# GpSimd starts one operation per step behind a VectorE gate; VectorE applies the softmax reciprocal in the first batch

## The chip, the cores and the metric

The kernel runs on one core of one Trainium2 chip. The metric is device time in microseconds. The engines are named PE (TensorE, matmul), PEld (its weight loads), DVE (VectorE), ACT (ScalarE), POOL (GpSimd) and SP (SyncE, which only issues DMAs here).

## What is computed

```python
q_pool = q.reshape(B, H, S // 2, 2, D).mean(axis=3)          # B 4, H 8, S 1152, D 64
scores = scale * np.matmul(q_pool, k.transpose(0, 1, 3, 2))
attn = np.exp(scores - np.max(scores, axis=-1, keepdims=True))
attn = attn / (np.sum(attn, axis=-1, keepdims=True) + 1e-09)
x = heads_side_by_side(np.matmul(attn, v))                   # [4, 576, 512]
xn = (x - mu) / np.sqrt(var + 1e-06) * g_ln
out = x + np.maximum(xn @ w_ch1, 0.0) @ w_ch2                # w_ch1 512 x 2048, w_ch2 2048 x 512
```

All inputs and the output are fp32. The kernel gets near fp32 precision from fp16 matmuls by splitting each operand into a high and a low half.

## The kernel before

The attention is cut into 144 **steps**. A step takes 128 query rows of one pair of heads; nine steps make a pair (`C = 9`), four pairs a batch, so steps 0 to 35 are the first batch (`on_pe(i)` is true there). The order of the work is written by hand: `step(i)` issues the instructions of step `i` engine by engine, and each engine runs its own list in that order, waiting only on semaphores. The dictionary `todo` (filled with `at(i, ...)`) holds what is issued at the end of step `i`, `early` (`pre(i, ...)`) what is issued at its start.

In a step of the first batch DVE begins with the row maximum of the scores in PSUM (`emit_max`, L381), takes the reciprocal of the softmax sum of an earlier step (`evac_pv`, L512), and then runs what waits in the queue `fill`: three integer operations on a 128 x 512 block of the weights (`w_conv`, recorded through a helper as L109), which turn fp32 words into a scaled form in SBUF. It ends with the low halves of the next pair's K or Q (L283, L306), read from PSUM. ACT makes the exponential (L395), copies the transposed exponentials out of PSUM (L434), multiplies the product with V by the reciprocal (`two` in `evac_pv`, L519) and makes the high halves. PE computes the scores (L362, L370), adds up the weights' magnitudes (L732), transposes the exponentials (L428), multiplies them by V (L452) and turns the result back (L480).

POOL has four jobs in the first batch: it adds pairs of query rows (`pool_q`, L172) and copies them (`dup_q`, L178) for every second pair, copies V (`take_v`, L273), and turns converted weights into two fp16 halves. The last is `w_splits(part)`: the weights come in four parts of four slots, and each slot takes three operations, `w_split_a` (fp32 to fp32, L257), `w_split_b` (to fp16, L257) and `w_split_c` (a difference, L788). A part is split once its scale is known, and then an operation is issued every half step or so. Nothing but its operands holds POOL back, so it runs them one behind the other.

From step 36 on, the feed-forward part (L600, L632) runs beside the attention of the later batches, as far as the weights' parts have been split.

```python
def w_splits(part):
    for n in range(4):
        i0 = this[0] + 1 + 3 * n // 2 if part < 2 else 16 + 10 * part + 5 * n // 2
        for x, fn in ((0, w_split_a), (1, w_split_b), (2, w_split_c)):
            at(i0 + x, fn, 4 * part + n)
```

Of the kernel before, what the change touches and what calls it, by code (L numbers as in the profile page):

```python
# [9 lines left out]
FP32 = mybir.dt.float32  # L10
# [4 lines left out]
ALU = mybir.AluOpType  # L15
# [9 lines left out]
def tile_pooled_attention_moe(  # L25
# [18 lines left out]
    nc = tc.nc  # L44
# [4 lines left out]
    C = S // 128  # L49
    HP = H // 2  # L50
# [18 lines left out]
    sm_p = ctx.enter_context(tc.tile_pool(name="sm", bufs=2))  # L69
# [97 lines left out]
    def pool_q(p, eng, halves=None):  # L167

        a = raws[p, "q"]
        for o, n in ((0, 128),) if halves is None else halves:  # L170
            x = a[o:o + n].rearrange("p h c r d -> p (h c) r d")
            eng.tensor_tensor(x[:, :, 0], x[:, :, 0], x[:, :, 1], op=ALU.add)  # L172

    def dup_q(p, eng, halves=None):
        a = raws[p, "q"]
        for o, n in ((0, 128),) if halves is None else halves:
            x = a[o:o + n].rearrange("p h c r d -> p (h c) r d")
            eng.tensor_copy(x[:, :, 1], x[:, :, 0])  # L178
# [45 lines left out]
    reds, found = deque(), deque()  # L224
# [31 lines left out]
    def scaled(dst, src, s=1.0):  # L256
        nc.gpsimd.tensor_scalar(dst, src, s, 1.0, op0=ALU.mult, op1=ALU.mult)  # L257

    def take_v(p, h):

        st = pair[p]
        vr = raws[p, "v"]
        if "v" not in st:

            st["v"] = tr_p.tile([128, 2, C, 130], FP16, tag="v", name="vt")
            if on_pe(p * C):
                st["v"] = st["v"].bitcast(FP32)
                nc.gpsimd.memset(st["v"][:, :, :, 64:65], 1.0)
            else:
                nc.gpsimd.memset(st["v"][:, :, :, 64:66], 1.0)  # L270
        vt = st["v"][:, h]
        if on_pe(p * C):
            nc.gpsimd.tensor_copy(vt[:, :, 0:D], vr[:, h])  # L273
            return
        s = st["s"][:, 2:3]
        scaled(vt[:, :, 0:D], vr[:, h], s)
        scaled(vr[:, h], vr[:, h], s)
        nc.gpsimd.tensor_tensor(vt[:, :, 66:66 + D], vr[:, h], vt[:, :, 0:D], op=ALU.subtract)
# [57 lines left out]
    def on_pe(i):  # L336

        return 0 <= i < HP * C
# [133 lines left out]
    turned, scaled_out = deque(), deque()  # L472

    def emit_turn(n, ot, i):

        j = n % C
        ps = psum[:, 3 * (i % 2) + 2, 128:258]
        parts = [(h, 64 * h, 64) for h in range(2)] if j == 4 else [(0, 0, 128)]
        for h, q0, w in parts:
            nc.tensor.transpose(ps[0:w, 65 * h:65 * h + 65], ot[:, q0:q0 + w], ident[0:65, 0:65])  # L480
        one, two = evac_pv(n, ps)
        found.append(one)
        scaled_out.extend((two, lambda: evacuated(n)))

    pv_slot = [0]
    xb, xh = {}, {}
# [1 line left out]
    def evac_pv(i, ps):  # L488

        p, j = divmod(i, C)  # L490
        b, hp = divmod(p, HP)
        s = pair[p]["s"][:, 2:3]
        r = sm_p.tile([128, 2], FP32, tag="r", name="r", bufs=3)
        if j == 4:
            if b % 2 == 0 and hp == 0:
                xh[b // 2] = x_p.tile([128, 2, DM], FP32, tag="hh", name="xh")
            o, n, m = 64 * (b % 2), 64, 2
            x = xh[b // 2][o:o + n, 0, 128 * hp:128 * hp + 128]
        else:
            if j == 0 and hp == 0:  # L500
                room["x"] -= 4
                assert room["x"] >= 0
                xb[b] = x_p.tile([128, 4, DM], FP32, tag="xb", name="xb")
            h, t = PLACES[hp // 2][j]
            o, n, m = 0, 128, 1
            x = xb[b][:, t, 128 * hp + 64 * h:128 * hp + 64 * h + 64]
        r = r[o:o + n, 0:m]

        def one():
            sums = ps[o:o + n, 64:65 * m:65]  # L510
            if on_pe(i):
                nc.vector.reciprocal(r, sums)  # L512
            else:
                nc.vector.tensor_scalar(r, sums, EPS, s[o:o + n], op0=ALU.add, op1=ALU.mult)
                nc.vector.reciprocal(r, r)  # L515

        def two():
            for u in range(m):
                nc.scalar.activation(  # L519
                    out=x[:, 64 * u:64 * u + 64], in_=ps[o:o + n, 65 * u:65 * u + 64],  # L520
                    func=ACTF.Copy, scale=r[:, u:u + 1],
                )

        return one, two
# [269 lines left out]
    def at(i, fn, *a):  # L794
        todo.setdefault(i, []).append((fn, a))
# [3 lines left out]
    def pre(i, fn, *a):  # L799
        early.setdefault(i, []).append((fn, a))  # L800
# [5 lines left out]
    for p in range(1, NP):  # L806
        i0 = (p - 1) * C
        at(max(i0 - 1, 0), load, p, "k", nc.sync)
        at(i0, load, p, "v", nc.sync)
        at(i0 + 1, bound, p, "k")  # L810
        if p % 2 == 0:
            at(i0 - 2, load_q, p, (nc.sync,))
            pre(i0 + 1, pool_q, p, nc.gpsimd)
            at(i0 + 1, dup_q, p, nc.gpsimd)
            at(i0 + 2, bound, p, "q")
        elif p == 1:
            upper = (64, 64)
            pre(0, behind_scales)
            pre(i0 + 1, pool_q, 1, nc.gpsimd, (upper,))
            at(i0 + 1, dup_q, 1, nc.gpsimd, (upper,))  # L820
            at(i0 + 2, bound, 1, "q", *upper)
        else:
            at(i0 + 1, same_q, p)
        if not on_pe(p * C):
            at(i0 + 2, bound, p, "v")
        pre(i0 + 3, scales_reduce, p, 0, 2 if on_pe(p * C) else 3)
        for n in range(2):
            at(i0 + (5, 7)[n], take_v, p, n)
        for n, (fn, u) in enumerate(PREPS):
            late = 1 if on_pe(i0) else 0  # L830
            pre(i0 + 4 + n + late, lambda fn=fn, p=p, u=u: preps.append((fn, p, u)))

    for m in range(32):
        i0 = m
# [5 lines left out]

    this = [0]

    def w_splits(part):
        for n in range(4):
            i0 = this[0] + 1 + 3 * n // 2 if part < 2 else 16 + 10 * part + 5 * n // 2
            for x, fn in ((0, w_split_a), (1, w_split_b), (2, w_split_c)):
                at(i0 + x, fn, 4 * part + n)

# [62 lines left out]
    def evacuated(n):  # L911

        p, j = divmod(n, C)
        b = p // HP
        left[p] -= 1
        if not left[p]:
            pair.pop(p)
        key = ("h", b // 2) if j == 4 else (b, PLACES[p % HP // 2][j][1])
        whole[key] = whole.get(key, 0) + 1
        if whole[key] == 8 and key != ("h", 0):  # L920
            norms.append(key)
# [34 lines left out]
    def step(i):  # L956
        live = i < NSTEP
        this[0] = i
        for fn, a in early.pop(i, ()):
            fn(*a)  # L960
        if live:
            emit_max(i)
        if on_pe(i - 1):
            emit_t_copy(i - 1)
            steps.pop(i - 1)
        while found:
            found.popleft()()
        first = on_pe(i - 2) or on_pe(i)
        if first and not on_pe(i):
            a_piece(i)  # L970
        if on_pe(i):
            if i < 3:
                warm(16, bank())
            a_piece(i)
            a_prep()
            emit_exp(i)
        while scaled_out:
            scaled_out.popleft()()
        if i + 1 < NSTEP:
            emit_s(i + 1)  # L980
            pv_slot[0] = i + 1
        else:
            free_banks[:] = [6, 7, 0, 1, 3, 4]
            pv_slot[0] += 1
        while sums and i % 2 == sums[0][0] // 2:
            sums.popleft()[1]()
        if on_pe(i):
            while fill:
                drip()
            flush()  # L990
        else:
            flush()
            if live:
                emit_exp(i)
                emit_hi(i)
        if 0 <= i - 1 < NSTEP and not on_pe(i - 1):
            emit_lo(i - 1)
            steps.pop(i - 1)
            drip()
        norm(i)  # L1000
        while soon or len(fill) > 3:
            drip()
        if on_pe(i):
            emit_t(i)
            if reds:
                found.append(reds.popleft()())
        elif reds:
            evacs.append(reds.popleft()())
        while turned:
            n, ot = turned.popleft()  # L1010
            emit_turn(n, ot, i)
        if not on_pe(i):
            if not first:
                a_piece(i)
            some_units(i)
            a_prep()
        for fn, a in todo.pop(i, ()):
            fn(*a)

    def warm(n, ps=None):  # L1020
        ps = psum[:, 2, 0:128] if ps is None else ps[:, 0:128]
# [3 lines left out]
    with tc.manual_schedule():  # L1025
# [36 lines left out]
        one, two = all_max(st["acc"], 3, lambda ps: scales(0, ps, 0, 3, both=True))  # L1062
# [13 lines left out]
        i = 0  # L1076
# [32 lines left out]
```

## Time and profile before

| | |
|---|---|
| time, median of 3 runs | 882.64 us (880.32 to 884.50) |
| the profiled execution: its own time | 883.46 us |
| its span on the core | 881.7 us |
| PE, PEld busy | 823.7 us (93%), 587.6 us (67%) |
| DVE, ACT, POOL busy | 614.7 us (70%), 570.7 us (65%), 349.0 us (40%) |
| the same from 0 to 204 us (the start and the first batch) | PE 182.84, DVE 161.55, ACT 160.82, POOL 70.61 us |

A span is the time from the first to the last instruction on the core. An instruction's duration is what the profiler recorded; short instructions of one engine overlap by some tens of nanoseconds. Steps are told apart by their row maximum: a step lasts from one L381 to the next.

### The profile page before, as it was taken

What the parts mean: (1) busy time and instruction counts of PE and PEld (TensorE: products, weight loads), DVE (VectorE), ACT (ScalarE), POOL (GpSimd) and SP (SyncE); (2) the same over time, 40 slices, a digit from 0 to 9 for tenths busy, and PEclk for the clock granted to TensorE, in tenths of its full rate; (3) what the DMA queues carried; (4) which work ended last, traced back from release to release, by engine and by line L of the source; (5) the groups of instructions that cost most, each with busy time, mean ns of one, the idle gap of its engine ahead of it and who ended that gap; (6) DMA issues with size and microseconds to landing.
All of it is one profiled execution on the core that took longest, in us unless ns stands there. A gap on an engine that the chain in (4) does not pass through costs nothing.

```text
span 881.7 us, 21840 instructions
## 1 busy us (share of the span) xinstructions
PE 823.7 (93%) x9270; PEld 587.6 (67%) x9270; DVE 614.7 (70%) x1092; ACT 570.7 (65%) x851; POOL 349.0 (40%) x318
## 2 busy tenths in 40 slices
PE   8999899898898999898899999999999999999997
PEld 6778687686656575556666666566757576666764
DVE  4687989897777787778778777777877777532121
ACT  3988788887566686668676767676768676411110
POOL 3010634436776934364464345526343423300000
PEclk9999989899999999999999999999999999999999
DMA  6463436303589698969697969796988967600001
GB/s 187 149 207 120 129 120 183 120 1 87 105 146 181 129 173 162 201 132 181 118 222 124 196 126 215 125 179 113 196 155 158 175 113 135 121 13 13 16 10 24
DMA packets 276017, 115.97 MB, mean 132 GB/s; under 512 B 259280, under 2 KB 259280, under 8 KB 275920
## 3 DMA queue, kind: packets, MB, share of 16 engines
q1 hardware_dynamic: 275568, 113.70, 62.3%
q8 instruction: 72, 1.18, 0.5%
q10 hardware_dynamic: 352, 0.88, 0.4%
q14 instruction: 25, 0.20, 0.1%
HBM read 46.14 MB, written 4.72 MB: 58 GB/s over the span
## 4 chain that ended last, share of the span: by engine, by line
PE 51%; DVE 26%; ACT 13%; DMA 4%; issue 3%; POOL 1%; SPq 1%; ACTq 0%; POOLq 0%; DVEq 0%
PE psum L632 15%; PE psum L600 14%; DVE mx L381 7%; PE psum L464 6%; DVE hl L418 5%; PE psum L362 4%; PE psum L452 4%; ACT pe L395 3%; DVE stage L109 3%; DVE ht L614 2%; PE psum L428 2%; ACT ht L613 2%; DVE wsl L109 2%; PE psum L370 2%; DVE kt L283 1%
## 5 line engine op out<-in xcount | busy, mean ns | idle before, releaser
L381 DVE TENSOR_REDUCE mx<-psum 128x1 f32<-128x1152 f32 x144 | 194.4, 1350 | 20.6 <-ACT xb L519 7.0
L632 PE MATMUL psum<-wsl,ht 128*128 128x512 f16 x864 | 196.6, 379 | 3.9 <-DVE ht L614 3.4
L395 ACT ACTIVATE pe<-psum,nb,sc 128x1152 f32<-128x1152 f32 x144 | 188.9, 1312 | 12.0 <-DVE nb L386 10.5
L600 PEld LDWEIGHTS <-wsl 128*128 128x128 f16 x1920 | 171.9, 99 | 29.5 <-issue 9.2
L600 PE MATMUL psum<-xn,wsl 128*128 128x256 f16 x1536 | 181.7, 277 | 8.4 <-DVE xb L645 4.3
L632 PEld LDWEIGHTS <-ht 128*128 128x128 f16 x864 | 80.8, 98 | 92.3 <-issue 4.5
L409 ACT ACTIVATE hl<-pe 128x1152 f16<-128x1152 f32 x108 | 125.6, 1163 | 8.0 <-DMA pt<-hl 4.7
L362 PE MATMUL psum<-kt,qt 64*128 64x512 f16 (+1 forms) x960 | 127.4, 381 | 1.7 <-ACT pe L395 0.9
L614 DVE SCALAR_TENSOR_TENSOR ht<-psum,ht 128x512 f16<-128x512 f32 x72 | 49.8, 691 | 104.7 <-ACT ht L613 104.7
L464 PE MATMUL psum<-vt,pt 128*128 128x65 f16 (+1 forms) x3240 | 117.6, 194 | 0.0
L464 PEld LDWEIGHTS <-pt 128*128 128x128 f16 (+1 forms) x3240 | 109.5, 100 | 2.5 <-DMA pt<-hl 0.4
L418 DVE SCALAR_TENSOR_TENSOR hl<-pe,hl 128x1152 f16<-128x1152 f32 x72 | 109.3, 1518 | 0.0
L519 ACT ACTIVATE xb<-psum,r 128x64 f32<-128x64 f32 x128 | 39.7, 310 | 96.1 <-DVE r L515 89.0
L613 ACT ACTIVATE ht<-psum 128x512 f16<-128x512 f32 x72 | 42.7, 593 | 88.2 <-PE psum L600 87.9
L257 POOL TENSOR_SCALAR pe<-pe 128x1152 f32<-128x1152 f32 x36 | 42.0, 1168 | 140.1 <-ACT hl L409 135.4
L416 POOL TENSOR_TENSOR hl<-pe,hl 128x1152 f16<-128x1152 f32 x36 | 85.5, 2374 | 3.0
L452 PE MATMUL psum<-pt,vt 128*65 128x128 f32 (+1 forms) x720 | 82.1, 272 | 1.4 <-DVE qt L283 1.4
L452 PEld LDWEIGHTS psum<-pt,vt 128*65 128x65 f32 x720 | 76.1, 144 | 1.8 <-DVE qt L283 1.8
L362 PEld LDWEIGHTS <-qt 64*128 64x128 f16 (+1 forms) x960 | 39.8, 97 | 39.7 <-issue 22.3
L370 PEld LDWEIGHTS <-qt 128*128 128x128 f16 (+1 forms) x320 | 17.8, 99 | 72.5 <-issue 72.0
L370 PE MATMUL psum<-kt,qt 128*128 128x128 f16 (+1 forms) x320 | 41.4, 226 | 12.1 <-ACT xb L519 10.6
L283 DVE SCALAR_TENSOR_TENSOR qt<-psum,s,qt 128x384 f16<-128x384 f32 x48 | 29.5, 614 | 33.3 <-ACT qt L286 33.2
(116 smaller groups left out, 1003.8 us busy)
## 6 DMA issues: line engine op xcount, KB each, us to landing
stage<-in_moe_w_ch_dram SPq DMA_DIRECT2D x32, 512.0 KB, 5.1
kr<-in_k_dram SPq DMA_DIRECT2D x16, 576.0 KB, 4.5
qr<-in_q_dram SPq DMA_DIRECT2D x31, 288.0 KB, 6.2
vr<-in_v_dram SPq DMA_DIRECT2D x15, 576.0 KB, 4.7
out_dram<-xb SPq DMA_DIRECT2D x32, 128.0 KB, 2.5
pt<-hl SPq DMA_TRANSPOSE x108, 4.9
kr<-in_k_dram SPq DMA_DIRECT2D x16, 64.0 KB, 4.2
vr<-in_v_dram ACTq DMA_DIRECT2D x1, 576.0 KB, 6.7
```

The lines of the kernel that those rows point to most:

```text
L362: nc.tensor.matmul(out=sp[o:o + w, c0:c0 + 512], lhsT=qt[r:r + 64, qa, q0:q0 + w], rhs=kt[r:r + 64, ka, h], start=(a == 0), stop=(a == 2),)
L370: nc.tensor.matmul(out=sp[o:o + w, 1024:1152], lhsT=qt[:, qa, q0:q0 + w], rhs=pair[p]["k8"][:, h], start=(qa == 0), stop=(qa == 1),)
L381: nc.vector.tensor_reduce(mx, st["s"], axis=AX.X, op=ALU.max)
L395: nc.scalar.activation(out=st["pe"], in_=st["s"], func=ACTF.Exp, scale=pair[i // C]["sc"][:, 0:1], bias=st["nb"],)
L409: nc.scalar.activation(out=hl[:, 0], in_=st["pe"], func=ACTF.Copy, scale=2.0 ** 15)
L416: nc.gpsimd.tensor_tensor(hl[:, 1], st["pe"], hl[:, 0], op=ALU.subtract)
L418: nc.vector.scalar_tensor_tensor(hl[:, 1], st["pe"], 2.0 ** 15, hl[:, 0], op0=ALU.mult, op1=ALU.subtract)
L452: nc.tensor.matmul(out=ps[0:65, q0:q0 + w], lhsT=vt[:, h, c], rhs=pt[:, 128 * u + q0:128 * u + q0 + w], start=(u == 0), stop=(u == C - 1),)
L464: nc.tensor.matmul(out=dst[:, 0:n], lhsT=lhsT, rhs=rhs, start=(u == 0 and lhsT is hi and n == 65), stop=(u == C - 1 and lhsT is lo), skip_ ...
L600: nc.tensor.matmul(out=ps[:, o:o + n], lhsT=wsl[:, 8 * w + cc, wa, f * 128:f * 128 + 128], rhs=xn[:, xa * KD + cc, 0:n], start=(m == 0), s ...
L614: lambda: nc.vector.scalar_tensor_tensor(lo, pv, 0.0, hi, op0=ALU.max, op1=ALU.subtract),
L632: nc.tensor.matmul(out=ps, lhsT=hv[0][:, ha, f, t * 128:t * 128 + 128], rhs=wsl[:, 8 * w + 4 + f // 2, wa, (f % 2) * DM:(f % 2) * DM + DM] ...
```

## The change

`gate()` is new: DVE writes one column of a small tile and POOL copies it to the next column. POOL runs in order, so what stands behind the copy on POOL starts only after DVE has come to that place. Four such tiles are used in turn.

```diff
+    def gate():
+        x = sm_p.tile([128, 2], FP32, tag="gate", name="gate", bufs=4)
+        nc.vector.memset(x[:, 0:1], 1.0)
+        nc.gpsimd.tensor_copy(x[:, 1:2], x[:, 0:1])
```

The splits of the weights' first two parts go into a queue, `calm`. At the end of each step up to 34 one gate and one operation of the queue are issued; from step 35 on two operations and no gate. The splits of parts 2 and 3 start three to four steps later. In the first batch the query addition and copy also go through the queue, ahead of the rest, their loads are issued two steps earlier, and V's copies get a gate each.

```diff
     def w_splits(part):
         for n in range(4):
-            i0 = this[0] + 1 + 3 * n // 2 if part < 2 else 16 + 10 * part + 5 * n // 2
+            if part < 2:
+                calm.extend((fn, 4 * part + n) for fn in (w_split_a, w_split_b, w_split_c))
+                continue
+            i0 = 22 + 9 * part + 5 * n // 2
...
         for fn, a in todo.pop(i, ()):
             fn(*a)
+        if calm and i < HP * C - 1:
+            gate()
+        for _ in range(1 if i < HP * C - 1 else 2):
+            if calm:
+                fn, n = calm.popleft()
+                fn(n)
...
         if p % 2 == 0:
-            at(i0 - 2, load_q, p, (nc.sync,))
-            pre(i0 + 1, pool_q, p, nc.gpsimd)
-            at(i0 + 1, dup_q, p, nc.gpsimd)
+            if on_pe(i0):
+                at(i0 - 4, load_q, p, (nc.sync,))
+                at(i0 - 1, lambda p=p: calm.appendleft((lambda n: pool_q(p, nc.gpsimd), 0)))
+                at(i0, lambda p=p: calm.appendleft((lambda n: dup_q(p, nc.gpsimd), 0)))
+            else:
...
         for n in range(2):
+            if on_pe(p * C):
+                at(i0 + (5, 7)[n], gate)
             at(i0 + (5, 7)[n], take_v, p, n)
```

The multiplication by the reciprocal moves from ACT to DVE in the first batch and stands directly behind the reciprocal, ahead of the exponential instead of behind it:

```diff
         one, two = evac_pv(n, ps)
-        found.append(one)
-        scaled_out.extend((two, lambda: evacuated(n)))
+        found.extend((one, two, lambda: evacuated(n)))
...
         def two():
             for u in range(m):
+                if on_pe(i):
+                    nc.vector.tensor_scalar(
+                        x[:, 64 * u:64 * u + 64], ps[o:o + n, 65 * u:65 * u + 64],
+                        r[:, u:u + 1], None, op0=ALU.mult,
+                    )
+                    continue
                 nc.scalar.activation(
```

POOL's list where the splits of part 0 and the second pair's V copies stand (`wsl` is the weights, `vt` V, `gs` the scale). Before:

```order
L788 TENSOR_TENSOR wsl<-wsl 128x1024
L257 TENSOR_SCALAR wsl<-wsl 128x1024
L788 TENSOR_TENSOR wsl<-wsl 128x1024
L257 TENSOR_SCALAR wsl<-wsl,gs_84 128x1024
L257 TENSOR_SCALAR wsl<-wsl 128x1024
L257 TENSOR_SCALAR wsl<-wsl,gs_84 128x1024
L788 TENSOR_TENSOR wsl<-wsl 128x1024
```

and with the change:

```order
L263 COPY gate<-gate 128x1
L257 TENSOR_SCALAR wsl<-wsl,gs_84 128x1024
L263 COPY gate<-gate 128x1
L257 TENSOR_SCALAR wsl<-wsl 128x1024
L263 COPY gate<-gate 128x1
L799 TENSOR_TENSOR wsl<-wsl 128x1024
L194 COPY acc<-acc 128x1
L263 COPY gate<-gate 128x1
L257 TENSOR_SCALAR wsl<-wsl,gs_84 128x1024
L263 COPY gate<-gate 128x1
```

Every split now has the gate's copy ahead of it, and one of them stands between two gates.

DVE's list in one step of the first batch, from one row maximum to the next. Before:

```order
L381 TENSOR_REDUCE mx<-psum 128x1
L512 RECIPROCAL r<-psum 128x1
L109 TENSOR_SCALAR stage<-stage 128x512
L109 SCALAR_TENSOR_TENSOR stage<-wsl,stage 128x512
L109 SCALAR_TENSOR_TENSOR wsl<-stage 128x512
L283 SCALAR_TENSOR_TENSOR qt<-psum,s,qt 128x384
L381 TENSOR_REDUCE mx<-psum 128x1
```

and with the change:

```order
L387 TENSOR_REDUCE mx<-psum 128x1
L517 RECIPROCAL r<-psum 128x1
L525 TENSOR_SCALAR xb<-psum,r 128x64
L109 TENSOR_SCALAR stage<-stage 128x512
L109 SCALAR_TENSOR_TENSOR stage<-wsl,stage 128x512
L109 SCALAR_TENSOR_TENSOR wsl<-stage 128x512
L289 SCALAR_TENSOR_TENSOR qt<-psum,s,qt 128x384
L262 MEMSET gate 128x1
L387 TENSOR_REDUCE mx<-psum 128x1
```

The multiplication (L525) has come in between the reciprocal and the conversion, and the gate's write (L262) right ahead of the next row maximum. PE's list is unchanged but for line numbers.

## Rows read from the trace of the kernel before

**Rows 1.** Stretches, of L109 on DVE alone: start:end length, busy (instructions), clock, DMA.
```profile
32.02:56.05 24.03, 9.01 (x15) 1.00 0.38 93
56.05:62.95 6.90, 5.05 (x3) 1.00 0.94 343
62.95:92.27 29.32, 10.73 (x18) 0.94 0.33 109
92.27:112.61 20.34, 13.38 (x9) 0.91 0.42 131
112.61:140.64 28.03, 11.53 (x18) 0.95 0.39 132
140.64:166.70 26.06, 17.16 (x12) 0.87 0.59 183
166.70:187.06 20.36, 7.16 (x12) 1.00 0.09 27
187.06:203.82 16.76, 8.49 (x9) 1.00 0.09 24
```

**Rows 2.** Timeline of DVE in step 26: start, duration, instruction.
```profile
146.86 1.34 DVE L381 TENSOR_REDUCE mx<-psum 128x1 f32<-128x1152 f32 x1
...
148.20 2.07 DVE L109 TENSOR_SCALAR stage<-stage 128x512 int32<-128x512 int32 x1
150.31 1.52 DVE L109 SCALAR_TENSOR_TENSOR stage<-wsl,stage 128x512 int32<-128x512 int32 x1
```

**Rows 3.** Timeline of POOL in the same step.
```profile
147.37 2.62 POOL L172 TENSOR_TENSOR qr<-qr 128x1152 f32<-128x1152 f32 x1
150.05 1.23 POOL L178 COPY qr<-qr 128x1152 f32<-128x1152 f32 x1
```

**Rows 4.** Stretches, all engines: length, busy of PE PEld DVE ACT POOL, clock, DMA.
```profile
105.00:110.00 5.00, 2.10 (x26) 1.34 (x25) 4.93 (x7) 2.31 (x5) 4.92 (x5) 0.88 0.42 161
110.00:115.00 5.00, 5.00 (x29) 5.00 (x27) 4.97 (x6) 3.05 (x6) 2.97 (x2) 0.50 0.63 206
...
112.61:140.64 28.03, 27.49 (x256) 22.94 (x255) 23.09 (x45) 24.70 (x47) 4.82 (x5) 0.95 0.39 132
```

**Rows 5.** The chain that ended last, two places: start, duration, piece.
```profile
65.97 0.21 ACT xb L519
...
67.83 3.65 PE psum L452 x18
...
127.68 1.97 PE psum L452 x18
```

**Rows 6.** Timeline of DVE in step 22, with what ended the idle time before.
```profile
126.49 1.36 DVE L381 TENSOR_REDUCE mx<-psum 128x1 f32<-128x1152 f32 x1
128.44 0.28 DVE L210 TENSOR_REDUCE mx<-psum 2x1 f32<-2x128 f32 x1 [0.59 <-ACT pt L434]
...
128.97 0.40 DVE L109 TENSOR_SCALAR stage<-stage 128x512 int32<-128x512 int32 x1
```

**Rows 7.** Timeline of DVE at 187 us.
```profile
186.96 0.18 DVE L546 BATCH_NORM_AGGREGATE mv<-bs 128x2 f32<-128x6 f32 x1
```

**Rows 8.** Timeline of POOL at 187 us.
```profile
187.22 0.19 POOL L551 TENSOR_SCALAR rs<-mv 128x1 f32<-128x1 f32 x1 [22.23 <-DVE mv L546]
```

**Rows 9.** POOL's groups from 0 to 204 us: busy, mean ns, idle before.
```profile
L788 POOL TENSOR_TENSOR wsl<-wsl 128x1024 f16<-128x1024 f32 x8 | 18.7, 2332 | 0.2
L257 POOL TENSOR_SCALAR wsl<-wsl 128x1024 f16<-128x1024 f32 x8 | 10.1, 1257 | 0.7
```

**Rows 10.** DVE's groups from 0 to 204 us: two that read few columns of PSUM.
```profile
L306 DVE SCALAR_TENSOR_TENSOR kt<-psum,s,kt 64x256 f16<-64x256 f32 x5 | 2.5, 491 | 0.8 <-ACT kt L311 0.7
...
L238 DVE TENSOR_SCALAR red<-psum 128x2 f32<-128x2 f32 x3 | 0.5, 159 | 2.4 <-ACT pt L434 2.4
```

**Rows 11.** PE's waits from 0 to 204 us: total, times, longest.
```profile
PE psum L370 <- ACT xb L519: 9.5, 9, 1.9
```

**Rows 12.** Timeline of SP's queue: the query load of the third and fourth pair.
```profile
46.45 2.39 SPq L137 DMA_DIRECT2D qr<-in_q_dram  x4
```

More of the change, by code (lines that the diff above doesn't have):

```diff
@@ L811, in tile_pooled_attention_moe @@
         if p % 2 == 0:
-            at(i0 - 2, load_q, p, (nc.sync,))
-            pre(i0 + 1, pool_q, p, nc.gpsimd)
-            at(i0 + 1, dup_q, p, nc.gpsimd)
+            if on_pe(i0):
[3 more added lines that the diff above has]
+            else:
+                at(i0 - 2, load_q, p, (nc.sync,))
+                pre(i0 + 1, pool_q, p, nc.gpsimd)
+                at(i0 + 1, dup_q, p, nc.gpsimd)
             at(i0 + 2, bound, p, "q")
@@ L841, in tile_pooled_attention_moe @@
     this = [0]
+    calm = deque()
     def w_splits(part):
         for n in range(4):
-            i0 = this[0] + 1 + 3 * n // 2 if part < 2 else 16 + 10 * part + 5 * n // 2
+            if part < 2:
+                calm.extend((fn, 4 * part + n) for fn in (w_split_a, w_split_b, w_split_c))
+                continue
+            i0 = 22 + 9 * part + 5 * n // 2
             for x, fn in ((0, w_split_a), (1, w_split_b), (2, w_split_c)):
```

## The prediction

> **What bounds the kernel now.** Over the whole span PE is busy 93%, so a gain must come from a place where PE waits or runs slowly. The clock row of the page's slices falls only early on, so I cut the first batch at its row maxima and asked for the weights' conversion (L109) alone [rows 1]. Each step from 4 to 35 converts one block in three instructions. In four of the stretches three instructions take 1.79 to 1.80 us (10.73 / 6, 9.01 / 5) and in a fifth 1.92; in the four others the same work takes 5.05, 4.46, 4.29 and 2.83 us. Taken at 1.79 a step, these four lose 3.3 + 8.0 + 10.0 + 3.1 us and the fifth 0.8, together **25 us of DVE**. They hold 11 steps (9, 16 to 18, 25 to 28, 33 to 35) of 70.06 us; the other 21 steps last 101.74 us, or 4.84 us each, and the fastest stretch among them 4.67.
>
> The cause stands in one step [rows 2, 3]. POOL's addition runs from 147.37 to 149.99 and the DVE operation that begins at 148.20 ends at 150.27; POOL's copy runs from 150.05 to 151.28 and the next DVE operation lasts 1.52 us, against some 0.69 undisturbed ((1.79 - 0.40) / 2) [rows 1, 6]. DVE comes out each time shortly after POOL's instruction ends: it waits for it. The row maximum of the same step reads PSUM, overlaps POOL by 0.8 us and takes 1.34 us, no more than the 1.36 of a step without POOL [rows 2, 6]. So a POOL operation under the row maximum costs DVE nothing, one under the conversion costs its remainder.
>
> PE pays twice. With DVE blocked PE is busy 2.10 of 5 us, and in the next 5 us its granted clock is 0.50, the lower level, 1.2 GHz [rows 4]. The product with V then takes 3.65 us instead of 1.97 [rows 5]. In an undisturbed stretch PE is busy 27.49 of 28.03 us [rows 4]: there PE is the bound, with DVE (23.09) and ACT (24.70) close behind.
>
> **The change part by part.** The sum is made on the profiled execution, 883.46 us; the median of the runs is 0.8 us lower.
>
> *Contention removed.* 70.06 us less 11 undisturbed steps at 4.75 us (between 4.67 and 4.84) is **-17.8 us**; with the two ends -18.7 and -16.8. It reaches the end of the kernel because PE's list is unchanged and what follows starts from the first batch's last step.
>
> *Clock.* Two products with V outside the disturbed steps run at the lower level, that of 67.83 us and the one just behind the second disturbed stretch, at the granted clock of 0.50; each costs 3.65 - 1.97 [rows 4, 5]. Without the stalls they don't: **-3.4 us** (0 if PE still starves somewhere).
>
> *When POOL now starts.* The gate's write is DVE's last instruction of a step. POOL woke 0.08 us after a DVE result (187.14 to 187.22), and its copy of one column should take about the 0.19 us of the row there [rows 7, 8]. So the operation begins some 0.3 us into the row maximum. The conversion begins 2.48 us after the maximum began in the step shown (128.97 - 126.49), because DVE waits 0.59 us for ACT's copy in between [rows 6]; without that wait it would be 1.9. A split of 1.26 us ends at 1.6 us: no collision. One of 2.33 us [rows 9] ends at 2.6 and can cost 0.1 to 0.7 us, a query addition of 2.62 [rows 3] up to 1.0. There are five such splits behind gates before step 35, two additions, and three steps in which two operations share the start of a step: ten collisions of about 0.3 us, half of it covered by DVE's wait for ACT: +1.5 us. V's preparation for the fifth pair and the layer norms at steps 31 to 34 have no gate; they are what POOL does in the last disturbed stretch, so most of its excess (16.76 - 3 x 4.75 = 2.5 us) stays: +2. Together **+3.5 us** (1 to 7).
>
> *DVE's new work.* A multiplication of 64 columns from PSUM isn't in the trace. Below it lies 0.16 us (2 columns), above it 0.49 (256 columns and a second operand) [rows 10]; between the two on a line 64 columns take 0.24, and without the second operand less, so I take 0.22. It must also wait for the reciprocal to finish, and the gate's write comes on top; the two together I put at half of another small operation (0.16). A step's DVE work grows by 0.3 us, in 33 steps by 10 us. Where DVE waits for ACT first, as in the step shown (0.59 us), this is hidden. In about one step of three, where pair scales or three low halves fall due, DVE has no such wait: **+4 us**. If the cover is missing everywhere it is +10, at 0.49 a multiplication about +18.
>
> The Trainium skill's Perfetto Trace Analysis, section Optimizing Scalar/DVE Operations, speaks against this part: it gives DVE a larger fixed cost on PSUM (about 125 ns) than ScalarE (51 ns), and advises to move work from a saturated DVE to ScalarE, not the other way. By its figure a multiplication would be an estimated 0.19 us, which no run here shows yet; by its advice the whole +10 would be paid, the second case below.
>
> *ACT's relief.* The multiplication leaves ACT's list behind the exponential. On the chain it is a piece of 0.21 us [rows 5], and PE's last score matmuls (L370) waited for it nine times, 9.5 us in all [rows 11]. Most of that wait covers the exponential, for which PE's transposes wait anyway. Left are the 0.2 us in about half of the steps and the matmuls that can now run earlier: **-3 us** (0 to -7).
>
> *Moved.* The query loads are issued two steps earlier, ahead of two weight loads on SP; their four issues take 2.4 us there [rows 12], and these weights are converted four steps later: nothing. POOL waits for DVE at every gate; behind it stand only splits, V and queries, which are needed steps later: nothing. DVE waits for POOL at a gate only if POOL is four gates late. POOL ends the first two parts about step 38, a few steps later than now, and parts 2 and 3 start three to four steps later, all before PE's list asks for them: nothing here, priced as rival 2.
>
> **Sum:** -17.8 - 3.4 + 3.5 + 4 - 3 = -16.7, so 866.8 on the profiled execution and **866 us** against the median.
>
> **Rivals.**
> 1. *DVE becomes the bound.* Its extra 0.3 us is paid in every step: +6 on the forecast, 872 us, and with a multiplication at the upper end 877. For: DVE and ACT trail PE by little [rows 4]. Against: DVE's wait for ACT in the undisturbed steps [rows 6].
> 2. *The gain is given back behind the first batch.* POOL's 24 splits of parts 2 and 3, at 1.3 to 2.3 us each [rows 9] some 39 us, now share steps 40 to 58 with the layer norms and the POOL-made low halves. Were four more steps of the second batch disturbed as the eleven are (16.8 / 11 = 1.5 us each), 6 us return; with rival 1's 6 to 11 on top about 880. For: the last disturbed stretch shows that POOL's V work collides as well [rows 1]. Against: the number of splits is the same, only later.
> 3. *The contention is spread, not removed,* and the kernel gets slower. If POOL's operation starts over 1 us later than I think, each of the 27 gated operations falls under the conversion. One collision costs about 0.8 us (1.52 - 0.69) [rows 2]: +22, with the DVE additions in full +10, the ungated rest +2 and ACT's relief -3, against -17.8: +13.6, or 896 us. It decides at a start 1.5 us into the row maximum. Against: POOL's wake of 0.08 us [rows 7, 8].
> 4. *PE alone is the bound afterwards:* the additions are all hidden and the clock stays up; -22 to -27, some 858 us.
>
> **How the numbers follow.** The forecast (860 to 871) gets 0.58, rival 1 (871 to 877) 0.19, rival 2 (878 to 885) 0.09, rival 3 0.06, rival 4 (852 to 860) 0.08. A measurement tells about 0.5% from no change, 4.4 us here. Faster by more than that: 0.58 + 0.19 + 0.08 = 0.85; the same 0.09; slower 0.06. The range from 855 to 877 leaves out rivals 2 and 3 and the end of rival 4, some 0.18.
>
> **What would show it.** Right: L109 means near 0.41, 0.69 and 0.69 us up to step 31 and excess left at steps 31 to 34; the row maximum of step 36 some 16 us earlier than 203.82; the granted clock at 1.00 from 60 to 165 us; POOL operations beginning 0.2 to 0.5 us after a row maximum; no wait of L370 for ACT's L519. Wrong: conversions of over 1 us in most gated steps (rival 3), DVE without idle time from step to step (rival 1), or a step 36 that is early and an end that isn't (rival 2).

## The result and the profile after

The changed kernel takes 870.0 us, median of 4 runs (868.66 to 872.36), beside 883.32 us (880.32 to 884.50) of the kernel before: a ratio of 0.986 [0.982, 0.989], 1.4% faster. The forecast was 866 us with a range of 855 to 877. The profiled execution took 868.78 us, 14.7 less than the one before.

Where the time came from is seen at the row maxima. Step 36 begins at 188.71 us, before at 203.82: 15.1 us earlier. The span is 866.9 us, before 881.7: 14.8 shorter. So nearly all of it is made before step 36, and 0.3 us is given back in the 678 us behind it. Here are the stretches of [rows 1], cut at the same steps, of L109 on DVE alone in the changed kernel (start:end length, busy, count, clock, DMA):

```profile
31.96:55.50 23.54, 9.03 (x15) 1.00 0.48 110
55.50:60.66 5.16, 2.60 (x3) 1.00 0.99 367
60.66:88.72 28.06, 10.84 (x18) 1.00 0.37 127
88.72:102.41 13.69, 5.47 (x9) 1.00 0.46 147
102.41:129.84 27.43, 11.14 (x18) 1.00 0.65 190
129.84:149.15 19.31, 8.57 (x12) 1.00 0.59 195
149.15:169.92 20.77, 7.24 (x12) 1.00 0.11 33
169.92:188.71 18.79, 8.57 (x9) 0.94 0.13 35
```

The three disturbed stretches before step 33 (rows two, four and six) fell from 6.90 + 20.34 + 26.06 = 53.30 us to 5.16 + 13.69 + 19.31 = 38.16. The conversions up to step 32 take 54.9 us together; at the undisturbed 1.80 a step, 29 steps would take 52.2. The clock is 1.00 in every row up to step 33, where four of [rows 1] have 0.87 to 0.95. The last stretch, steps 33 to 35, went the other way: 18.79 us, before 16.76.

One step tells how. DVE and POOL in step 21 of the changed kernel, two timelines (start, duration, instruction):

```profile
111.50 1.35 DVE L387 TENSOR_REDUCE mx<-psum 128x1 f32<-128x1152 f32 x1
...
113.07 0.28 DVE L525 TENSOR_SCALAR xb<-psum,r 128x64 f32<-128x64 f32 x1
113.27 0.42 DVE L109 TENSOR_SCALAR stage<-stage 128x512 int32<-128x512 int32 x1
```
```profile
111.66 0.18 POOL L263 COPY gate<-gate 128x1 f32<-128x1 f32 x1 [3.19 <-DVE gate L262]
111.81 1.04 POOL L257 TENSOR_SCALAR wsl<-wsl 128x1024 f16<-128x1024 f32 x1
```

POOL's copy wakes 0.16 us after the row maximum begins, its split starts 0.31 us after it and ends at 112.85, as the row maximum does. The conversion behind it takes its undisturbed 0.42 us, and it starts 0.20 us after the multiplication does. A query addition is too long for this window. Step 27 of the changed kernel, DVE and then POOL:

```profile
139.37 1.35 DVE L387 TENSOR_REDUCE mx<-psum 128x1 f32<-128x1152 f32 x1
...
141.03 1.59 DVE L109 TENSOR_SCALAR stage<-stage 128x512 int32<-128x512 int32 x1
```
```profile
139.71 2.62 POOL L172 TENSOR_TENSOR qr<-qr 128x1152 f32<-128x1152 f32 x1
```

POOL ends at 142.33 and DVE's 0.42 us operation comes out at 142.62, 1.2 us late. It is the largest collision left before step 33. (The window, from the row maximum's start to the conversion, is 1.66 us in the shortest steps and over 2 us in about two of three.)

PE's side, by stretches of all engines (length, busy of PE, PEld, DVE, ACT and POOL, clock, DMA): the changed kernel from the start of step 4 to that of 33, from 33 to 36 and from 36 to 56.

```profile
31.96:169.92 137.96, 135.84 (x1360) 113.07 (x1361) 122.62 (x279) 123.22 (x210) 34.57 (x52) 1.00 0.47 143
169.92:188.71 18.79, 15.58 (x160) 12.81 (x159) 16.72 (x31) 11.75 (x22) 15.82 (x22) 0.94 0.13 35
188.71:297.81 109.10, 95.03 (x1112) 64.24 (x1111) 85.00 (x145) 72.73 (x97) 89.30 (x67) 0.99 0.71 132
```

The same three of the kernel before:

```profile
32.02:187.06 155.04, 141.69 (x1358) 119.72 (x1359) 132.94 (x224) 129.17 (x242) 48.92 (x34) 0.94 0.40 126
187.06:203.82 16.76, 14.66 (x163) 12.19 (x162) 15.65 (x24) 12.90 (x26) 12.67 (x16) 1.00 0.09 24
203.82:311.59 107.77, 95.92 (x1098) 64.13 (x1095) 81.25 (x141) 73.44 (x100) 81.05 (x63) 0.97 0.72 135
```

Of the 17.1 us gained in steps 4 to 33, 11.2 are idle time of PE (13.35 to 2.12) and 5.9 are its busy time, at a clock of 1.00 instead of 0.94. PE is now busy 98% of this stretch. DVE's 132.94 us held the blocked time, its 122.62 hold the multiplications instead. And the wait of PE's last score matmuls for the multiplication, 9.5 us in [rows 11], is down to 0.5. PE's largest wait up to 189 us in the changed kernel, and that one (total, times, longest):

```profile
PE psum L434 <- ACT pe L401: 4.6, 9, 0.9
...
PE psum L376 <- DVE xb L525: 0.5, 1, 0.5
```

### The profile page after: what moved, and what is told of

The parts are those of the page before. It is cut to its first block, busy times and chain, and to the rows that moved or that the text cites. A ratio compares the mean times of both kernels' runs of the same rounds, so it can differ in the third digit from the quotient of the medians.

```text
span 866.9 us, 21890 instructions
## 1 busy us (share of the span) xinstructions
PE 814.4 (94%) x9270; PEld 579.8 (67%) x9270; DVE 609.7 (70%) x1159; ACT 562.5 (65%) x811; POOL 348.5 (40%) x345
## 4 chain that ended last, share of the span: by engine, by line
PE 51%; DVE 24%; ACT 10%; DMA 7%; issue 3%; POOL 2%; SPq 2%; ACTq 0%; POOLq 0%; DVEq 0%
PE psum L643 15%; PE psum L611 14%; DVE mx L387 7%; PE psum L470 5%; DVE hl L424 5%; PE psum L368 5%; PE psum L458 5%; DMA qr<-in_q_dram 3%; PE psum L434 3%; DVE ht L625 2%; ACT pe L401 2%; ACT ht L624 2%; DMA vr<-in_v_dram 2%; DMA pt<-hl 2%; PE psum L376 2%
## 5 line engine op out<-in xcount | busy, mean ns | idle before, releaser
L611 PEld LDWEIGHTS <-wsl 128*128 128x128 f16 x1920 | 169.6, 98 | 26.9 <-issue 9.0
L611 PE MATMUL psum<-xn,wsl 128*128 128x256 f16 x1536 | 176.8, 273 | 8.3 <-DVE xb L656 4.9
L424 DVE SCALAR_TENSOR_TENSOR hl<-pe,hl 128x1152 f16<-128x1152 f32 x72 | 112.6, 1564 | 0.0
L257 POOL TENSOR_SCALAR pe<-pe 128x1152 f32<-128x1152 f32 x36 | 44.1, 1226 | 134.6 <-ACT hl L415 134.6
L530 ACT ACTIVATE xb<-psum,r 128x64 f32<-128x64 f32 x96 | 29.8, 310 | 95.4 <-DVE r L520 82.6
L422 POOL TENSOR_TENSOR hl<-pe,hl 128x1152 f16<-128x1152 f32 x36 | 85.4, 2372 | 3.0
L458 PE MATMUL psum<-pt,vt 128*65 128x128 f32 (+1 forms) x720 | 78.2, 264 | 1.9 <-DVE qt L289 1.9
L458 PEld LDWEIGHTS psum<-pt,vt 128*65 128x65 f32 x720 | 72.2, 139 | 2.4 <-DVE qt L289 2.4
L440 ACT COPY pt<-psum 128x512 f32<-128x512 f32 x72 | 44.9, 638 | 10.1 <-PE psum L434 4.8
L263 POOL COPY gate<-gate 128x1 f32<-128x1 f32 x27 | 5.2, 191 | 113.8 <-DVE gate L262 113.8
```

The lines of the kernel that those rows point to most:

```text
L422: nc.gpsimd.tensor_tensor(hl[:, 1], st["pe"], hl[:, 0], op=ALU.subtract)
L424: nc.vector.scalar_tensor_tensor(hl[:, 1], st["pe"], 2.0 ** 15, hl[:, 0], op0=ALU.mult, op1=ALU.subtract)
L458: nc.tensor.matmul(out=ps[0:65, q0:q0 + w], lhsT=vt[:, h, c], rhs=pt[:, 128 * u + q0:128 * u + q0 + w], start=(u == 0), stop=(u == C - 1),)
L611: nc.tensor.matmul(out=ps[:, o:o + n], lhsT=wsl[:, 8 * w + cc, wa, f * 128:f * 128 + 128], rhs=xn[:, xa * KD + cc, 0:n], start=(m == 0), s ...
```

## The experiments

The theory: DVE's weight conversion was blocked by POOL's SBUF operations, and the gate gains by letting POOL begin where DVE reads PSUM. Its rivals: that the multiplication's move from ACT makes the gain; that the queue, which spreads the splits and loads queries earlier, makes it without a gate; that PE's clock makes it. Behind these stood what the multiplication costs DVE, and what the splits cost that now come later. All stretches below run from row maximum to row maximum ("steps 4 to 33" ends where step 33 begins); step 36 begins the second batch. Each group of runs had the kernel before beside it, at 882.0 to 882.8 us. Diffs are against the changed kernel unless said otherwise.

**The gates without the multiplication.**

```diff
-        found.extend((one, two, lambda: evacuated(n)))
+        found.append(one)
+        scaled_out.extend((two, lambda: evacuated(n)))
...
-                if on_pe(i):
-                    nc.vector.tensor_scalar(
...
-                    continue
```

> The changed kernel with the multiplication by the reciprocal back on ACT, behind the exponential. Theory A (the gates alone make the gain, the multiplication is about neutral: +4 on DVE, -3 on ACT): 869 us, 867 to 872, within 0.3% of the changed kernel; PE's L370 waits for ACT's multiplication again, some 5 to 9 us in all, hidden behind the exponential. Theory B (the multiplication off ACT's list makes half of the gain or more, because PE's score matmuls no longer wait for it): 876 to 880 us.

Measured: 870.36 us, ratio 0.987 [0.984, 0.990]. Steps 4 to 33, PE's largest wait, and two undisturbed stretches of L109:

```profile
33.52:175.03 141.51, 134.77 (x1358) 113.11 (x1359) 116.14 (x247) 128.24 (x242) 34.66 (x52) 1.00 0.45 138
```
```profile
PE psum L376 <- ACT xb L525: 7.1, 9, 0.9
```
```profile
62.74:91.84 29.10, 10.76 (x18) 1.00 0.35 117
...
106.40:134.05 27.65, 11.71 (x18) 1.00 0.63 183
```

Steps 4 to 33 are 13.5 us shorter than before, steps 33 to 35 0.8 longer (17.57): the first batch is 12.7 us shorter, most of the change. The clock is up throughout, yet the four undisturbed stretches sum to 101.85 us (24.05 + 29.10 + 27.65 + 21.05), before 101.74 [rows 1]. The two shown here are those that had a clock of 0.94 and 0.95 before: they take 56.75 us, before 57.35, so the clock gives them little.

**The multiplication without the gates.** The two edits taken out above, put into the kernel before.

> The kernel before with only the multiplication moved to DVE, directly behind the reciprocal. Theory A: the conversion is disturbed as before (L109 about 82 us in all); DVE's extra 0.32 us costs some 3.5 us in the 11 disturbed steps, where DVE is the bound, ACT's relief gives back 3: 882 to 885 us. Theory B: 874 to 878 us.

Measured: 883.46 us, 1.002 [1.000, 1.005]; steps 4 to 33 take 155.30 us, before 155.04. By itself it is worth nothing: the undisturbed steps of [rows 1] take 1.4 us less (100.34), the disturbed ones up to step 33 1.7 more (54.96).

**The queue without the gate.**

```diff
     def gate():
-        x = sm_p.tile([128, 2], FP32, tag="gate", name="gate", bufs=4)
-        nc.vector.memset(x[:, 0:1], 1.0)
-        nc.gpsimd.tensor_copy(x[:, 1:2], x[:, 0:1])
+        return
```

> The changed kernel with gate() doing nothing: the queue still puts one split a step on POOL's list, but nothing holds POOL back, so it runs ahead as before. Theory A (the gate is what keeps POOL out of the conversion): L109 70 to 85 us in all and 879 to 886 us. Theory C (spreading the splits or loading the queries two steps earlier makes the gain): L109 about 63 us and 868 to 872 us.

Measured: 883.1 us, 1.002 [0.999, 1.004]. POOL's timeline in this kernel:

```profile
93.78 1.12 POOL L257 TENSOR_SCALAR wsl<-wsl,gs 128x1024 f32<-128x1024 f32 x1 [20.66 <-DVE r L515]
94.98 1.10 POOL L257 TENSOR_SCALAR wsl<-wsl 128x1024 f16<-128x1024 f32 x1
96.16 2.45 POOL L797 TENSOR_TENSOR wsl<-wsl 128x1024 f16<-128x1024 f32 x1
```

The queue puts one operation at the end of a step into POOL's list, but POOL doesn't see where steps end: the three run one behind the other. Spreading, early loads and the multiplication, all of it there, gain nothing without something that holds POOL back. The conversions of the first batch do take less in sum (75.5 us, before 82.5), yet steps 4 to 33 last 155.88 us. Much of that stands in two steps in which POOL begins a query addition as soon as its load has landed, without a gate: step 5 with 7.68 us and step 23 with 10.34, 5.36 each in the change. In step 23 POOL's operations also lie over three of DVE's small operations on the pair's scales (L243, L246, L252), which take 1.17, 1.10 and 1.01 us there and 0.17, 0.17 and 0.15 in step 5, where they are undisturbed; L109's sum doesn't hold these.

**The gate half a step later.** The gate and one operation stand behind the row maximum, the reciprocal and the multiplication, right ahead of the conversion:

```diff
+        if calm and i <= HP * C - 1:
+            gate()
+            fn, n = calm.popleft()
+            fn(n)
...
-        if calm and i < HP * C - 1:
-            gate()
-        for _ in range(1 if i < HP * C - 1 else 2):
-            if calm:
-                fn, n = calm.popleft()
-                fn(n)
+        if i >= HP * C - 1:
+            for _ in range(2):
+                if calm:
+                    fn, n = calm.popleft()
+                    fn(n)
```

> The changed kernel with the gate and its one POOL operation issued half a step later: behind the row maximum, reciprocal and multiplication, right ahead of the conversion. Theory A (what counts is that POOL's operation lies under an operation that reads PSUM): each of about 24 operations now delays the conversion by 0.8 to 1.2 us, so L109 takes 82 to 92 us in all and the kernel 882 to 895 us. Theory C (one operation a step is what counts, wherever in the step): L109 about 63 us and 868 to 872 us.

Measured: 882.36 us, 1.000 [0.998, 1.002]. DVE and POOL in one of its steps, and L109 over steps 4 to 33:

```profile
116.38 0.06 DVE L262 MEMSET gate<- 128x1 f32 x1
116.82 1.54 DVE L109 SCALAR_TENSOR_TENSOR stage<-wsl,stage 128x512 int32<-128x512 int32 x1
```
```profile
116.78 1.04 POOL L257 TENSOR_SCALAR wsl<-wsl 128x1024 f16<-128x1024 f32 x1
```
```profile
34.31:186.90 152.59, 76.98 (x87) 1.00 0.43 130
```

The same gates, one a step, in another place: the conversions take 77.0 us instead of the change's 54.9, as much as before (74.0 over the first seven of [rows 1]), and nearly all of the gain is gone. The place makes it, not the spreading. And these 152.59 us pass at a clock of 1.00, so a blocked DVE alone holds the steps up, and the clock is no rival.

The lengths agree with what the Trainium skill's SBUF — State Buffer, section Who interferes with whom, says of these two engines: where an instruction of DVE needs the port that POOL uses too, the one that comes second waits until the first's instruction is done, and a reduction never contends on trn2. The row maximum under POOL's split shows it here, at 1.35 us with POOL and 1.36 without [rows 6].

**The splits behind the first batch.** The splits wait until step 35 and then go out three a step; queries and V keep their gates.

```diff
-        if calm and i < HP * C - 1:
+        if calm and i < HP * C - 1 and calm[0][0] not in (w_split_a, w_split_b, w_split_c):
             gate()
-        for _ in range(1 if i < HP * C - 1 else 2):
+            fn, n = calm.popleft()
+            fn(n)
+        for _ in range(0 if i < HP * C - 1 else 3):
...
-            i0 = 22 + 9 * part + 5 * n // 2
+            i0 = 24 + 9 * part + 5 * n // 2
```

> The changed kernel with the first two parts' 24 splits moved behind step 34, three a step from step 35 on without gates (parts 2 and 3 start two steps later; one feed-forward unit of PE moves by a step). POOL then splits nothing under the conversion. Theory A (the gated splits cost next to nothing in the first batch, what is left of the contention stands in steps 33 to 35): from step 4 to step 36 it takes 151 to 155 us against 156.75 of the changed kernel, and POOL's splits then pile up in steps 35 to 43, so the whole takes 868 to 876 us. Theory D (the gated splits still cost several us, in collisions or at the gates): under 150 us from step 4 to 36.

Measured: 877.93 us, 0.995 [0.993, 0.997]. Steps 4 to 33, 33 to 36 and 36 to 56 of this kernel:

```profile
33.18:171.08 137.90, 135.78 (x1360) 113.03 (x1361) 121.86 (x266) 123.32 (x210) 13.13 (x24) 1.00 0.46 142
171.08:187.62 16.54, 14.49 (x161) 11.96 (x160) 15.18 (x28) 11.75 (x22) 10.87 (x16) 1.00 0.08 22
187.62:305.48 117.86, 96.37 (x1088) 65.63 (x1085) 84.18 (x145) 72.55 (x97) 111.11 (x81) 0.96 0.64 125
```

With no split in steps 4 to 33 these take 137.90 us, with the gated ones 137.96: here the gated splits cost nothing. Steps 33 to 35 fall to 16.54 without splits. But from 36 to 56 POOL is busy 111 of 118 us and 8.8 us are lost to the change's 109.10, so the whole lies some 8 us above the change's 870.0, about 2 beyond what was expected. This is rival 2's case, once enough splits pile up, though not only by blocking DVE: ACT waits 10.0 us there, in two waits, for the low halves that POOL makes (L422), a wait that the change doesn't have.

**Fewer splits at the seam, in two ways.** The first keeps one gated operation a step up to step 41 (`HP * C + 6` in both places for `HP * C - 1`), the second issues no split in steps 32 to 35 and keeps a gate a step behind:

```diff
+        late = 32 <= i < 36
-        if calm and i < HP * C - 1:
+        if calm and not late:
             gate()
-        for _ in range(1 if i < HP * C - 1 else 2):
+        for _ in range(0 if late else 1 if i < 36 else 2):
```

Both start the last two parts two steps later (`24 + 9 * part`).

> The changed kernel with one gated split a step up to step 41 instead of two ungated ones from step 35 on (parts 2 and 3 start two steps later). If contention in steps 35 to 41 is worth anything: 867 to 869 us. If those steps have another bound, or the splits only meet DVE's low halves (L424) later: 870 to 872 us.

> The changed kernel without splits in steps 32 to 35, where POOL also prepares V and normalizes; from step 36 on one gate and two splits a step. If the splits are what makes steps 33 to 35 long (18.79 us for three): those take 16 to 17 us and the kernel 867 to 869 us. If V's preparation and the norms do it alone: 18 to 19 us, and 869 to 872 us.

> One gated split a step up to step 41 again, beside the changed kernel. If the contention behind step 33 is worth 2 us: 866 to 869 us and 1 to 4 us below the changed kernel of this group; if not, within 1 us of it.

Measured: 867.44 us, 0.983 [0.980, 0.986], for the first and 867.3, 0.983 [0.981, 0.986], for the second; the first again, on the same chip as the change again, 869.19, 0.986 [0.983, 0.988]. The change there took 868.21. Steps 33 to 36 of the second:

```profile
170.41:186.95 16.54, 14.48 (x161) 11.96 (x160) 15.17 (x27) 11.74 (x22) 10.46 (x15) 1.00 0.08 21
```

It saves 2.3 us at the seam. What is left of them later isn't settled: its step 57 begins 267.7 us after its step 4, in the change's two traces 269.6 and 268.8 us after, and its step 70 335.9 us after, in the change 337.9 and 335.1. The intervals of the times overlap. No version better than the change is shown.

**The multiplication twice.** The same instruction again, into a scratch tile:

```diff
+                    y = sm_p.tile([128, 64], FP32, tag="twice", name="twice", bufs=1)
+                    nc.vector.tensor_scalar(
+                        y[o:o + n], ps[o:o + n, 65 * u:65 * u + 64],
+                        r[:, u:u + 1], None, op0=ALU.mult,
+                    )
```

> The changed kernel with DVE's multiplication done twice, the second into a scratch tile that nobody reads: 40 more operations of 0.28 us, some 0.2 us apart. If DVE's work is mostly hidden under its wait for ACT's copy (PE is the bound): 870 to 873 us. If DVE has become the bound (my rival 1): 0.2 to 0.28 us in each of 36 steps, 877 to 881 us.

Measured: 872.58 us, 0.988 [0.986, 0.991]. DVE in one of its steps, and steps 4 to 33 and 33 to 36:

```profile
114.14 0.28 DVE L525 TENSOR_SCALAR xb<-psum,r 128x64 f32<-128x64 f32 x1
114.34 0.27 DVE L530 TENSOR_SCALAR twice<-psum,r 128x64 f32<-128x64 f32 x1
114.53 0.42 DVE L109 TENSOR_SCALAR stage<-stage 128x512 int32<-128x512 int32 x1
```
```profile
32.09:171.98 139.89, 136.53 (x1362) 113.58 (x1363) 127.84 (x312) 122.22 (x210) 34.57 (x52) 1.00 0.47 141
171.98:191.55 19.57, 15.82 (x158) 12.85 (x157) 17.05 (x35) 11.67 (x21) 16.61 (x22) 0.91 0.14 38
```

The second multiplication takes 0.20 us from start to start, and the 37 of them from step 4 to 36 make 7.4 us of DVE. The path pays 1.9 and 0.8 of it, 2.7 us: some third. So DVE has room for most of it and isn't the bound.

**Two splits behind one gate.** `w_split_a` and `w_split_b` go out together, `w_split_c` alone; none at the end of steps 32 and 34, and one gate with each from step 36 on.

```diff
-                calm.extend((fn, 4 * part + n) for fn in (w_split_a, w_split_b, w_split_c))
+                calm.extend(((lambda n: (w_split_a(n), w_split_b(n)), 4 * part + n), (w_split_c, 4 * part + n)))
```

> The changed kernel with the first two operations of a split behind one gate, so that a slot takes two steps instead of three, none at the ends of steps 32 and 34 and one gate with each from step 36 on. The pair lasts 1.1 + 1.0 us behind the gate, as long as the third operation alone, which was seen to cost nothing. If so: the steps up to 33 unchanged (138 us from step 4), steps 33 to 35 under 17.5 us, the kernel 866 to 868 us. If pairs do collide with the conversion: L109 over 65 us in all and 870 us or more.

Measured: 872.22 us, 0.989 [0.986, 0.991]; steps 4 to 33 take 141.12 us. One pair, DVE and POOL:

```profile
115.11 1.35 DVE L387 TENSOR_REDUCE mx<-psum 128x1 f32<-128x1152 f32 x1
116.78 1.18 DVE L109 TENSOR_SCALAR stage<-stage 128x512 int32<-128x512 int32 x1
```
```profile
115.43 1.12 POOL L257 TENSOR_SCALAR wsl<-wsl,gs 128x1024 f32<-128x1024 f32 x1
116.63 1.05 POOL L257 TENSOR_SCALAR wsl<-wsl 128x1024 f16<-128x1024 f32 x1
```

The window is 1.67 us long here, from the row maximum to the conversion (115.11 to 116.78). One split fits, the second ends 0.9 us behind it, and DVE comes out 0.3 us after that, 0.76 late. But the pairs are not alone. `w_split_c`, by itself behind its gate, is too long for a short step as well, as in step 18 of this kernel (POOL, then DVE):

```profile
101.82 2.13 POOL L799 TENSOR_TENSOR wsl<-wsl 128x1024 f16<-128x1024 f32 x1
```
```profile
103.17 1.05 DVE L109 TENSOR_SCALAR stage<-stage 128x512 int32<-128x512 int32 x1
```

The conversion here comes out 0.63 us late. The change issues one operation a step, and its four such splits before step 33 fall into steps 19, 22, 25 and 30, with windows of 2.02, 2.85, 2.63 and 4.24 us; only the first collides, by 0.28 us. That they cost next to nothing there is luck of the order, and the expectation's premise, that the third operation was seen to cost nothing, doesn't hold in a short step.

**The change and the gates alone, again, on one chip.**

> The changed kernel itself, to stand beside the other three on the same chip: 868 to 872 us.

> The gates alone again, the multiplication on ACT, beside the changed kernel. If the multiplication on DVE is worth the 2 to 3 us by which the first batch was shorter in one trace: 871 to 874 us, above the changed kernel of this group. If it is neutral: within 1.5 us of it.

Measured: the change 868.21 us, 0.985 [0.982, 0.987]; the gates alone 870.6, 0.987 [0.985, 0.989]. Steps 4 to 33 of the change again, and of the gates alone again:

```profile
32.33:170.32 137.99, 135.85 (x1360) 113.07 (x1361) 122.64 (x280) 123.28 (x210) 34.67 (x52) 1.00 0.46 142
```
```profile
31.73:173.25 141.52, 134.77 (x1358) 113.12 (x1359) 116.15 (x248) 128.24 (x242) 34.66 (x52) 1.00 0.45 138
```

The gates alone came out 2.4 us above the change, which is over the 1.5 us of the neutral case and short of the 871 us of the other. The intervals overlap, so the times alone don't separate the two. The stretches do: 137.96 and 137.99 us against 141.51 and 141.52.

## Why the prediction was right

The direction and the cause held, and the sum came close: -16.7 us was forecast for the profiled execution and -14.7 measured. How close is in part luck, because two terms were off by 3.4 and 3.3 us in opposite directions. The terms, each against a run that holds it alone:

| term | forecast | measured | by |
|---|---|---|---|
| contention, steps 4 to 33, with the new collisions | -15.3 + 1.5 | -13.5 | the gates alone |
| steps 33 to 35 | -2.5 + 2 | +0.8 | the gates alone, 16.76 to 17.57 |
| clock | -3.4 | some -0.6, held in the first row | the gates alone |
| multiplication: DVE's new work and ACT's relief | +4 - 3 | -2.3 | the change less the gates alone |
| behind the first batch | 0 | +0.3 | span and step 36 |

**Contention removed** held to 0.3 us. A step of the gates alone takes 141.51 / 29 = 4.88 us, near the undisturbed 4.84 of [rows 1]. The gate's start was taken at 0.3 us into the row maximum and is 0.31, so rival 3 (1.5 us) was far. Up to step 33 not ten operations collided but five: the two query additions by 1.5 us each, one split by 1.0 and two by some 0.2, with the gates alone. That the place in the step makes it, and not the spreading, is shown by the gate half a step later and by the queue without a gate.

**The clock term failed.** "each costs 3.65 - 1.97" and "Without the stalls they don't" took the whole 1.68 us of each slow product off the path. Both products lie in undisturbed stretches, those of 29.32 and 28.03 us in [rows 1]. At a clock of 1.00 the same steps take 29.10 and 27.65 with the gates alone: 0.6 us less for both, with 0.2 us more of conversions in them. The first product's step, 11, fell from 5.08 to 4.36 us, and step 12 grew from 6.29 to 6.77. So most of a slow product was hidden. What holds these steps instead stays open.

**Steps 33 to 35** were mis-sized. "Most of its excess stays: +2" left a small gain; the stretch grew by 0.8 with the gates and by 2.0 with the change. The prediction named V's preparation and the layer norms as what POOL does there, and passed over a split: the longest conversion of the stretch, in step 34 of the kernel before, waits for the last split of part 1 (POOL, then DVE).

```profile
192.94 2.13 POOL L788 TENSOR_TENSOR wsl<-wsl 128x1024 f16<-128x1024 f32 x1
```
```profile
193.04 2.31 DVE L109 TENSOR_SCALAR stage<-stage 128x512 int32<-128x512 int32 x1
```

With the change three splits of the queue fall into these steps, where before there was this one. Two of them, and DVE:

```profile
175.80 2.12 POOL L799 TENSOR_TENSOR wsl<-wsl 128x1024 f16<-128x1024 f32 x1
178.22 1.63 POOL L257 TENSOR_SCALAR wsl<-wsl,wscl 128x1024 f32<-128x1024 f32 x1
```
```profile
176.95 1.25 DVE L109 TENSOR_SCALAR stage<-stage 128x512 int32<-128x512 int32 x1
178.97 1.42 DVE L109 SCALAR_TENSOR_TENSOR wsl<-stage 128x512 int32<-128x512 int32 x1
```

DVE's two operations, 0.42 and 0.69 undisturbed, wait for these splits. With the splits taken out of steps 33 and 34 the three steps last 16.54 us.

**The multiplication** was right in what it costs (0.22 us taken, 0.20 measured) and wrong in the sum of its two terms, +1 against -2.3. The doubling shows that some third of such work is paid, 2.7 us. If the first one costs the same, ACT's relief is some -5 and not -3; that division is an estimate, only the net is measured. The multiplication also lengthens the window for POOL (1.34 us in the shortest steps of the gates alone, 1.66 in the change), but that isn't where the gain comes from: the three steps in which POOL collides most, 9, 19 and 27, take the same in both (5.17, 4.63 and 5.46 us; 5.16, 4.63 and 5.47). The relief is seen at PE: its last score matmuls wait 7.1 us for ACT's multiplication with the gates alone and 0.5 with the change, and PE's idle time in steps 4 to 33 falls from 6.74 to 2.12 us. Rival 1, the whole 10 us paid, isn't borne out.

The Trainium skill's Perfetto Trace Analysis, section Optimizing Scalar/DVE Operations, says that moving work from DVE to ACT may make sense where DVE is saturated, and gives no price for a move the other way. DVE was the fuller of the two over the whole span (70% against ACT's 65%), but 70% is not saturated, so the prediction's "by its advice the whole +10 would be paid" asks more of the page than it states. In steps 4 to 33 of the gates alone, where the move gains 3.5 us, DVE is busy 116.14 of 141.51 us and ACT 128.24, so in the stretch that counts ACT was the fuller one. The estimated 0.19 us by the page's figure agrees with the 0.20 measured from start to start (0.28 recorded).

**Rival 2** is small in the change (+1.3 us in steps 36 to 56, most of it made up later) and real when it is forced, as the splits behind the first batch show. **Rival 4** has its state, PE busy 98% of steps 4 to 33 at a clock of 1.00, but not its time: these steps gave 17.1 us, not 22 to 27, with next to nothing from the clock.

What stays open: whether the change is faster than the gates alone in time. The traces say 2.3 us of the first batch, and the times agree (868.21 and 870.6) without showing it.

## What to carry to other kernels

Where two engines block each other on SBUF, look for the instruction of one that reads only PSUM, and let a one-column write at its start release one operation of the other: the place of the start counts, a queue in program order alone does nothing. Size the window first (here 1.66 us in the shortest steps, enough for a split of 1.1 us and too short for two or for one of 2.1), and count what is pushed behind it. Price the removal of a stall by the undisturbed length of the whole step, and take a slow matmul's extra time off only where a step is seen to be longer for it.

## What was not expected

In the changed kernel's profile the whole gate costs little: 27 copies on POOL, 5.2 us in all, and a DVE write of 0.06 us that lies under the row maximum's start.

```profile
L263 POOL COPY gate<-gate 128x1 f32<-128x1 f32 x27 | 5.2, 191 | 113.8 <-DVE gate L262 113.8
```

With the gate at the conversion, the clock stayed at 1.00 over 152.59 us although DVE was blocked as much as before; PE was busy 140.70 of these us. The lower clock of [rows 1] came with stalls bunched in a few steps; one short stall a step didn't bring it here.
